# When the output weights' combinations are made in the value stage: units 0 to 3 in place of units 1 to 4

## The chip, the cores and the metric

The kernel runs on one core of one Trainium2 chip. The metric is the device time of one execution in microseconds (us). Engines are named as in the profile: PE (TensorE matmuls), DVE (VectorE), ACT (ScalarE), POOL (GpSimd) and SP (SyncE, which issues most DMAs).

## The reference, cut to what matters

The input is one sequence of 2048 tokens with 1024 features. The output is a gated sum of two blocks of the same input:

```python
g = _sigmoid((x * gate_w).sum(-1, keepdims=True))
a = _A_ref(x, A_wqkv, A_wo)                    # attention: 32 heads of width 32, softmax over 2048 keys
b = _B_ref(x, B_w_q, B_k1, B_k2, B_u, B_v)     # product-key experts, one of 64 for each of 32 heads
return g * a + (1 - g) * b
```

What concerns us here is inside `_A_ref`: the values `v = x @ wqkv[:, 2048:]` (2048x1024 by 1024x1024), and, at the very end, `o @ wo` (2048x1024 by 1024x1024). All matrices are float32.

## The kernel before, in words

**Precision.** Every operand of a large matrix product is split in two parts: ACT copies it to a reduced type (the high part), DVE subtracts that from the original (the low part). That is `split` (line 94; ACT works in line 95, DVE in line 96). A product is then three matmuls for every 128 rows of depth: high by high, high by low, low by high (line 964). So the third matmul of a product is the first that needs the low part of its left operand, and the first one needs its high part.

**Seven products in place of eight.** A block of 256 tokens by 1024 features by 1024 output columns is computed by a Winograd form of Strassen's scheme: both operands are cut into quarters (A11, A12, A21, A22 of the tokens; B11 to B22 of the weights), sums of quarters are made (S1 to S4 of the tokens, T1 to T4 of the weights), and seven products P1 to P7 take the place of eight. Each product is 12 matmuls of 128x128 by 512 columns into one bank of PSUM. DVE then adds the products up to the four quarters C11, C12, C21, C22 of the result.

**Stages.** The kernel first makes queries and keys, then the expert router, then the values (the value stage), then attention over 32 heads (by far the longest part), and finally the output product with `wo`. The output product also uses the scheme with seven products, and so it needs T1 to T4 of `wo`. These do not depend on the data of the other stages. They are made ahead of time during the value stage and are written to DRAM (the tensors `t0h` to `t3l`), from where the last stage reads them back.

**The value stage.** The last 512 tokens are done by plain products before it. The other 1536 are six units of 256 tokens (`values_unit(u)`, line 1144, u = 0 to 5, called from line 1230). The order of the products is P1, P2, P3, P7, P5, P6, P4 in unit 0, and P1, P7, P5, P6, P2, P3, P4 in units 1 to 4. Inside a unit the code is a loop over these seven (k = 0 to 6). All engines work in the order of this code, each on its own list, and an instruction that waits holds up all behind it on its engine. In the loop stand:

- after P1: ACT copies P1 out of PSUM (`c1`, line 1165), and SP issues `load_x_raw(u + 2)`, the 1 MB of tokens of the unit after the next (the *token load*). It goes to one of two buffers, `xw` and a half of the tile `xl`.
- after P6: four sums of products on DVE, then C11 after P2, C12 after P3, C21 after P4 (line 970). Each result goes to DRAM by a DMA that SP issues (`vd`, line 1152).
- the operands of the *next* unit: the high and low parts of A11, the four sums S3, S1, S2, S4 (line 946), and then the splits of S3, S1, S2, A12, S4 and A22, each as soon as the product of this unit that used the same buffer is done. In unit 0 the split of A11 and the sums come at k = 4, the other splits from k = 5 on. In later units they come at k = 0 and from k = 1 on. In the trace the splits that read A11 and A12 write the tile `a`, those of S1 to S4 write `xh`, and that of A22 writes `vo`.
- the *weight work*, which is what the change moves: `load_early(i)` (line 1118) issues four DMAs of 256 KB each on SP (four blocks of `wo`, into the other half of the tile `xl`), `sums_early()` (line 1123) is four sums in place on DVE, and `split_early(i, j)` (line 1130), for j = 0 to 3, is one split each, after which POOL's queue writes both parts to DRAM (`t0h`, `t0l`, `t2h`, `t2l`, `t3h`, `t3l`, `t1h`, `t1l`). There are four rounds, i = 0 to 3. They share one buffer: the load of the next round overwrites what the writes of the last one read. The first sum needs two of the four pieces of a load, the second sum needs the piece that is issued last.

**Banks.** `bank()` (line 110) hands out the eight PSUM banks in turn. A unit takes seven. After each unit up to the fifth one number is left out (line 1241), so that P1 of a unit gets the bank of P1 of the unit before. Between units 1 and 2 there is an exception: `peer_turn` (line 1041) makes four tiles of transposes there, which take four banks more. P1 of unit 2 therefore gets the bank that P2 had in unit 1, and P2's bank becomes free with the sum C11. `peer_turn` also sends four DMAs on SP (`atd<-z`). After their landing, the keys and queries of the first head are loaded by SP (`z<-kdh` and the following ones), and a DVE memset of the same buffer waits for them too (line 1236).

Of the kernel before, what the change touches and what calls it, by code (L numbers as in the profile page):

```python
# [20 lines left out]
HC = KC // 2  # L21
# [10 lines left out]
def gated_mha_peer_kernel(ctx, tc, xT, wqkv, wv, wo, wq, k12, ug, v, out):  # L32
# [42 lines left out]
    def dma(dst, src, queue=nc.sync):  # L75
        a, b = (ap.bitcast(F32) if ap.dtype == F32R else ap for ap in (dst, src))
        return queue.dma_start(a, b)
# [16 lines left out]
    def split(hi, lo, src, on=None):  # L94
        nc.scalar.activation(hi, src, AF.Copy)
        (on or nc.vector).tensor_tensor(out=lo, in0=src, in1=hi.bitcast(F32), op=OP.subtract)
# [872 lines left out]
    def tt(out, a, b, op=OP.add):  # L969
        nc.vector.tensor_tensor(out=out, in0=a, in1=b, op=op)  # L970
# [108 lines left out]
    def load_x_raw(u):  # L1079
        dma(x_raw[u % 2], xT[:, u * W:(u + 1) * W].rearrange("(k p) m -> p k m", p=128))  # L1080
# [37 lines left out]
    def load_early(i):  # L1118
        for j in range(4):
            c0 = (i + j // 2 * HC) * D + j % 2 * 512  # L1120
            dma(early[:, j], wo_rows[:, :, c0:c0 + 512])

    def sums_early():
        b11, b12, b21, b22 = (early[:, j] for j in range(4))
        tt(b11, b12, b11, OP.subtract)
        tt(b12, b22, b12, OP.subtract)
        tt(b22, b22, b11, OP.subtract)
        tt(b21, b21, b22, OP.subtract)

    def split_early(i, j):  # L1130
        hi, lo = work[f"th{j}"].bitcast(F32R), early[:, j].bitcast(F32R)
        split(hi, lo, early[:, j])
        for part, t in enumerate((hi, lo)):

            dma(TD[(0, 2, 3, 1)[j]][part][:, i, :], t, nc.gpsimd)
# [8 lines left out]
    def values_unit(u):  # L1144
        c1, u2, u3, u5 = (work[k] for k in ("c1", "u2", "u3", "u5"))
        last = u == NU - 1
        order = (("P1", "P2", "P3", "P7", "P5", "P6", "P4") if u == 0 else
                 ("P1", "P7", "P5", "P6", "P3", "P2", "P4") if last else
                 ("P1", "P7", "P5", "P6", "P2", "P3", "P4"))
        p, done = {}, set()  # L1150

        def out(j, half, t, queue=nc.sync):
            dma(VD[half][(2 * u + j) * 128:(2 * u + j + 1) * 128, :], t, queue)

        for k, name in enumerate(order):
            if last and name == "P4":

                nonlocal pso
                ps1.close()
                pso = Pool("pso", space=PSUM, side="right")  # L1160
            p[name] = hv.product(name, bank=pv_bank if last and name == "P4" else None)
            if last and name == "P2":
                first_scores()
            if name == "P1":
                nc.scalar.activation(c1, p[name], AF.Copy)
                hv.rows(x_raw[(u + 1) % 2])
                if u + 2 < NU:
                    load_x_raw(u + 2)
            if name == "P6":
                tt(u2, c1, p["P6"])  # L1170
                tt(u3, u2, p["P7"])
                tt(u2, u2, p["P5"])
                tt(u5, u3, p["P5"])
                out(1, 1, u5)
            if "P6" in p:
                if "P2" in p and "C11" not in p:
                    p["C11"] = tt(c1, c1, p["P2"])
                    out(0, 0, c1)
                if "P3" in p and "C12" not in p:
                    p["C12"] = tt(u2, u2, p["P3"])  # L1180
                    out(0, 1, u2)
            if name == "P4":
                tt(u3, u3, p["P4"])

                out(1, 0, u3, nc.gpsimd if last else nc.sync)

            if u + 1 < NU:
                if k == (4 if u == 0 else 0):
                    hv.parts("A11")
                    for s in ("S3", "S1", "S2", "S4"):  # L1190
                        hv.sums(s)
                    done = {"P1"}
                if k >= 5 or u > 0:
                    for q in ("P7", "P5", "P6", "P2", "P3", "P4"):
                        if q in p and q not in done:
                            hv.parts(hv.FACTORS[q][0])
                            done.add(q)
            if 1 <= u <= HC:
                if k == 0:
                    load_early(u - 1)  # L1200
                if k == 3:
                    sums_early()
                for j in {4: (0,), 5: (1,), 6: (2, 3)}.get(k, ()):
                    split_early(u - 1, j)

    P, pools = {}, {}

# [7 lines left out]
    def first_scores():  # L1215

        tp.close()
        pools.update(right=Pool("ppr", side="right"), next=0)
        K, Q = Z
        pt = p_tile(0, 0)  # L1220
        for qc, i in enumerate((5, 6, 0, 1)):
            ps = ps1.tile([128, 512], F32, name=f"bk{i}")
            c = slice(qc * 512, (qc + 1) * 512)
            nc.tensor.matmul(ps, K[:98, :128], Q[:98, c], start=True, stop=True)
            nc.scalar.activation(pt[:, c], ps, AF.Exp, scale=SCALE)
# [4 lines left out]
    for u in range(NU):  # L1230
        values_unit(u)
        if u == 1:
            peer_turn(Ahl)
            for i in range(2):
                Z[i] = zp.tile([128, S], F32R, name=f"z{i}")
            nc.vector.memset(Z[0][96:98, :].bitcast(F32), 1.0)
            load_kq(0, Z)
            load_shift(0, Z)

        if u < 5:  # L1240
            bank_no[0] += 1
# [207 lines left out]
    for h in range(H):  # L1449
        base = h * NT  # L1450
        g, j = divmod(h, 4)
# [319 lines left out]
```

## Time and profile before

| | us |
|---|---|
| median of 3 runs (range) | 1825.43 (1825.37 to 1826.04) |
| the profiled execution, its own time | 1824.19 |
| its span in the trace | 1822.4 |
| value stage, unit 0's first product to unit 5's last scores | 497.48 to 613.94 |
| one unit of seven products | 19.3 |
| PE busy / DVE busy / ACT busy in the span | 1814.7 / 1461.8 / 1312.8 |

The profiled execution's own time is 1.8 us above its span, and 1.2 us below the median of the runs. The timeline rows show, from the left: start, duration, engine, line, operation, the tiles (out<-in), the shape, and how many instructions are merged in the row; a bracket at the end holds idle time before it and what ended that. Consecutive matmuls overlap in such rows, so the time from one start to the next is their rate: 12 matmuls in 2.79 us.

### The profile page before, as it was taken

How to read it: one execution, taken by the hardware profiler on the slowest of the kernel's cores; microseconds unless marked ns; L12 is line 12 of the kernel's file. 1: busy time of each engine (PE TensorE's matmuls, PEld its weight loads, DVE VectorE, ACT ScalarE, POOL GpSimd, SP SyncE). 2: the span in 40 equal slices, each digit the busy share in tenths (PEclk: the TensorE clock that was granted, in tenths of full speed). 3: DMA queues.
4: the chain of work that ended last, by engine and by line, in shares of the span. 5: the costliest groups of instructions: out<-in, count | busy, mean ns of one | idle time of the engine just before them, and what ended most of it. 6: DMA issues, size and time to landing. Idle time of an engine off the chain costs nothing.

```text
span 1822.4 us, 26410 instructions
## 1 busy us (share of the span) xinstructions
PE 1814.7 (100%) x10083; PEld 1099.5 (60%) x10083; DVE 1461.8 (80%) x1258; ACT 1312.8 (72%) x1716; POOL 227.5 (12%) x351
## 2 busy tenths in 40 slices
PE   9999999999999999999999999999999999999999
PEld 6777777788888644444444444444444444447887
DVE  7865876689967888888888888888888888897674
ACT  5544544532333699999999999999999999994221
POOL 1222222244101100000000000000000000000000
PEclk9999999999999999999999999999999999999999
DMA  7888689560267778777788878878787777866641
GB/s 268 277 280 277 215 291 292 191 224 13 81 231 239 232 161 183 157 168 167 166 173 174 181 163 178 171 171 185 165 182 168 163 167 179 185 149 243 252 156 58
DMA packets 117504, 345.23 MB, mean 189 GB/s; under 512 B 16160, under 2 KB 50112, under 8 KB 96448
## 3 DMA queue, kind: packets, MB, share of 16 engines
q1 hardware_dynamic: 87176, 195.37, 36.0%
q0 software_dynamic: 27888, 145.00, 34.4%
q10 hardware_dynamic: 2312, 3.15, 0.5%
q8 instruction: 80, 1.31, 0.3%
q14 instruction: 48, 0.39, 0.1%
HBM read 171.76 MB, written 72.36 MB: 134 GB/s over the span
## 4 chain that ended last, share of the span: by engine, by line
PE 94%; issue 2%; DVE 2%; DMA 1%; ACT 0%; POOL 0%; ACTq 0%; SPq 0%; DVEq 0%; POOLq 0%
PE ring L1318 29%; PE o L1339 26%; PE bk L303 15%; PE pa L964 6%; PE bk L725 5%; PE pa L1521 2%; PE bk L983 2%; PE bk L291 2%; PE bk L964 2%; PE bk L342 2%; PE ring L1352 1%; PE pa L1528 1%; DVE xh L970 1%; DMA t1l<-xl 0%; PE bk L191 0%
## 5 line engine op out<-in xcount | busy, mean ns | idle before, releaser
L1328 ACT ACTIVATE P<-ring 128x1024 f32<-128x1024 f32 (+2 forms) x1031 | 913.0, 984 | 13.3
L1368 DVE TENSOR_TENSOR acc<-acc,P 128x2048 f32<-128x2048 f32 x319 | 731.0, 2292 | 73.3 <-ACT P L1328 48.0
L1339 PE MATMUL o<-P,V 128*32 128x512 f32 x3840 | 464.8, 599 | 0.0
L1318 PE MATMUL ring<-Q,K 98*128 98x512 f32 x1024 | 271.7, 407 | 0.1
L1318 PE MATMUL ring<-z,z 98*128 98x512 f32 x1020 | 270.5, 407 | 0.6 <-ACT accd L1328 0.6
L1318 PEld LDWEIGHTS ring<-Q,K 98*128 98x128 f32 x1024 | 182.2, 188 | 143.6 <-ACT P L1328 73.5
L1318 PEld LDWEIGHTS ring<-z,z 98*128 98x128 f32 x1020 | 181.6, 188 | 142.3 <-ACT P L1328 72.3
L1339 PEld LDWEIGHTS o<-P,V 128*32 128x32 f32 x3840 | 99.0, 109 | 223.3 <-issue 214.4
L1361 POOL DMA_DIRECT2D accd<-P x95 | 81.5, 858 | 928.6 <-PE ring L1318 321.6
L1366 DVE TENSOR_TENSOR acc<-P,P 128x2048 f32<-128x2048 f32 x32 | 73.4, 2293 | 73.8 <-ACT P L1328 73.8
L303 PE MATMUL bk<-xh,A 128*128 128x512 f32 x336 | 82.8, 396 | 0.0
L303 PE MATMUL bk<-xh,S 128*128 128x512 f32 x336 | 81.3, 393 | 0.0
L303 PE MATMUL bk<-xl,S 128*128 128x512 f32 x336 | 80.1, 391 | 0.0
L136 ACT ACTIVATE hi<-u 128x512 fp32r<-128x512 f32 x42 | 26.6, 632 | 70.2 <-issue 39.7
L303 PEld LDWEIGHTS bk<-xh,A 128*128 128x128 f32 x336 | 62.1, 188 | 23.8 <-issue 5.9
L1371 DVE TENSOR_TENSOR acc<-acc,accd 128x2048 f32<-128x2048 f32 x32 | 73.1, 2285 | 0.0
L303 PEld LDWEIGHTS bk<-xl,S 128*128 128x128 f32 x336 | 62.8, 188 | 16.3 <-issue 2.5
L303 PEld LDWEIGHTS bk<-xh,S 128*128 128x128 f32 x336 | 62.4, 188 | 14.5 <-issue 1.7
L1328 ACT ACTIVATE accd<-ring 128x1024 f32<-128x1024 f32 (+2 forms) x64 | 62.3, 1034 | 2.3 <-PE ring L1318 2.2
L964 PE MATMUL pa<-woh,acc 128*128 128x512 f32 x192 | 62.2, 389 | 0.0
L512 DVE TENSOR_TENSOR u<-u,bk 128x512 f32<-128x512 f32 x70 | 46.7, 683 | 10.0 <-DMA wpd<-u 5.6
L729 ACT ACTIVATE xu<-bk 128x64 f32<-128x64 f32 x16 | 3.6, 222 | 61.1 <-PE bk L725 61.1
(301 smaller groups left out, 2209.3 us busy)
## 6 DMA issues: line engine op xcount, KB each, us to landing
accd<-P POOLq DMA_DIRECT2D x95, 1024.0 KB, 7.8
wqt<-in_wq SPq DMA_DIRECT2D x64, 512.0 KB
wraw<-in_wqkv SPq DMA_DIRECT2D x28, 512.0 KB
kdh<-hi POOLq DMA_DIRECT2D x32, 256.0 KB, 5.3
kdl<-lo POOLq DMA_DIRECT2D x32, 256.0 KB, 6.5
qdh<-hi POOLq DMA_DIRECT2D x32, 256.0 KB, 6.0
qdl<-lo POOLq DMA_DIRECT2D x32, 256.0 KB, 5.8
z<-kdh SPq DMA_DIRECT2D x32, 256.0 KB
```

The lines of the kernel that those rows point to most:

```text
L291: nc.tensor.matmul(b0[w, n], AW[PLAIN[w, ki]][a][:, k, :], X[f"B{ki + 1}{n + 1}"][b][:, k, :], start=first, stop=last)
L303: nc.tensor.matmul(ps, a[i][:, k, :], b[j][:, k, :], start=(k == 0 and i == j == 0), stop=(k == HC - 1 and i == 1))
L512: nc.vector.tensor_tensor(out=out, in0=a, in1=b, op=OP.add)
L725: nc.tensor.matmul(ps, x_part(a, t // 4, kc)[:, tok], b, start=first, stop=last)
L964: nc.tensor.matmul(ps, self.a[a][i][:, k, :], self.b[b][j][k], start=(not first and k == 0 and i == j == 0), stop=(k == HC - 1 and i == 1))
L1318: on_ring(nc.tensor.matmul(ring[:, i, :], K[:98, kt * 128:(kt + 1) * 128], Q[:98, qc * 512:(qc + 1) * 512], start=True, stop=True), i)
L1328: on_ring(nc.scalar.activation(P[h, kt][:, q0 * 512:(q0 + m) * 512].rearrange("p (a m) -> p a m", a=m), ring[:, i:i + m, :], AF.Exp, scale ...
L1339: nc.tensor.matmul(O[h][32 * qc:32 * qc + 32, :], Vt[g][:, kt, 32 * j:32 * j + 32], p[:, qc * 512:(qc + 1) * 512], start=(kt == 0), stop=( ...
L1361: nc.gpsimd.dma_start(ACCD[h], P[h, kt], accum_op=OP.add)
L1366: nc.vector.tensor_add(ACC[h], P[h, 0], P[h, kt])
L1368: nc.vector.tensor_add(ACC[h], ACC[h], P[h, kt])
L1371: nc.vector.tensor_add(ACC[h], ACC[h], ACCD[h])
```

## The change

The weight work is done in units 0 to 3 in place of 1 to 4. In the loop of `values_unit`, for unit u, the round is now u, and no longer u - 1:

```diff
-            if 1 <= u <= HC:
+            if u < HC:
                 if k == 0:
-                    load_early(u - 1)
+                    load_early(u)
                 if k == 3:
                     sums_early()
                 for j in {4: (0,), 5: (1,), 6: (2, 3)}.get(k, ()):
-                    split_early(u - 1, j)
+                    split_early(u, j)
```

`HC` is 4. The number of instructions is the same on every engine. Only their order changes, and, for unit 0, their place between the instructions of that unit's own loop order: the four sums come at k = 3, which in unit 0 is after P7 in the code and *ahead* of the split of A11 for unit 1 (k = 4).

The DMA list of SP around unit 0 before the change. `in_xT` are the token loads for units 1, 2 and 3, `vd` the results of unit 0, and the last row is the first load of `wo`:

```order
L77 DMA xl_4614<-in_xT 128x8x256
L77 DMA xw<-in_xT 128x8x256
L77 DMA vd_68<-xh_4594 128x512
L77 DMA vd_67<-xh_4594 128x512
L77 DMA vd_68<-xh_4594 128x512
L77 DMA vd_67<-xh_4594 128x512
L77 DMA xl_4614<-in_xT 128x8x256
L77 DMA xl_4614<-in_wo 128x1x512 x4
```

The same place after the change, up to the second load of `wo`:

```order
L77 DMA xl_4614<-in_xT 128x8x256
L77 DMA xw<-in_xT 128x8x256
L77 DMA xl_4614<-in_wo 128x1x512 x4
L77 DMA vd_68<-xh_4594 128x512
L77 DMA vd_67<-xh_4594 128x512
L77 DMA vd_68<-xh_4594 128x512
L77 DMA vd_67<-xh_4594 128x512
L77 DMA xl_4614<-in_xT 128x8x256
L77 DMA xl_4614<-in_wo 128x1x512 x4
```

A first load of `wo` now stands right behind the token loads for units 1 and 2, ahead of unit 0's results.

DVE's list of unit 0 before, from the low part of A11 for unit 1 (`a_4458`) over the sums S3, S1, S2, S4 (L946) and the sums of products (L970 with a bank `bk`) to the low parts of S3 and S1 (the last row):

```order
L96 TENSOR_TENSOR a_4458<-xl_4614,a_4458 128x512
L946 TENSOR_TENSOR xh_4594<-xl_4614 128x512 x2
L946 TENSOR_TENSOR xl_4614<-xh_4594,xl_4614 128x4x128
L946 TENSOR_TENSOR xl_4614<-xl_4614 128x4x128
L970 TENSOR_TENSOR xh_4594<-xh_4594,bk_4690 128x512
L970 TENSOR_TENSOR xh_4594<-xh_4594,bk_4658 128x512
L970 TENSOR_TENSOR xh_4594<-xh_4594,bk_4671 128x512 x2
L970 TENSOR_TENSOR xh_4594<-xh_4594,bk_4632 128x512
L970 TENSOR_TENSOR xh_4594<-xh_4594,bk_4645 128x512
L96 TENSOR_TENSOR xh_4582<-xh_4594,xh_4582 128x512 x2
```

The same stretch of DVE's list after the change:

```order
L970 TENSOR_TENSOR xl_4614<-xl_4614 128x512 x4
L96 TENSOR_TENSOR a_4458<-xl_4614,a_4458 128x512
L946 TENSOR_TENSOR xh_4594<-xl_4614 128x512 x2
L946 TENSOR_TENSOR xl_4614<-xh_4594,xl_4614 128x4x128
L946 TENSOR_TENSOR xl_4614<-xl_4614 128x4x128
L96 TENSOR_TENSOR xl_4614<-xl_4614,xh_4594 128x512
L970 TENSOR_TENSOR xh_4594<-xh_4594,bk_4702 128x512
L970 TENSOR_TENSOR xh_4594<-xh_4594,bk_4662 128x512
L970 TENSOR_TENSOR xh_4594<-xh_4594,bk_4679 128x512 x2
L970 TENSOR_TENSOR xh_4594<-xh_4594,bk_4636 128x512
L970 TENSOR_TENSOR xh_4594<-xh_4594,bk_4649 128x512
L96 TENSOR_TENSOR xh_4582<-xh_4594,xh_4582 128x512 x2
```

Two pieces of weight work stand in it now: the four sums of `wo` at its head (the first row), and the low part of the first split ahead of the sums of products (the sixth row).

## The prediction

> **What bounds the kernel now.** I read the head of the page first, then the chain that ended last, then PE's waits in the value stage, and only then the engines' lists there.
>
> ```profile
> span 1822.4 us, 26410 instructions
> PE 1814.7 (100%) x10083; PEld 1099.5 (60%) x10083; DVE 1461.8 (80%) x1258; ACT 1312.8 (72%) x1716; POOL 227.5 (12%) x351
> PE 94%; issue 2%; DVE 2%; DMA 1%; ACT 0%; POOL 0%; ACTq 0%; SPq 0%; DVEq 0%; POOLq 0%
> ```
>
> PE is busy for 1814.7 of 1822.4 us, and the chain is 94% PE. The change takes no matmul away. So it can win only what PE waits now, and lose whatever new waits it makes for PE. PE's waits between 470 and 640 us, which hold the value stage and the start of attention (waited for; us in total, times, longest):
>
> ```profile
> PE ring L1318 <- ACT accd L1328: 0.6, 1, 0.6
> PE bk L1224 <- DVE xh L970: 0.5, 1, 0.5
> ```
>
> Both lie behind unit 5. Units 0 to 5 themselves run without a wait, so moving the weight work earlier has at most 1.1 us to win, and only if both vanish. What it can lose is the question. The PE rows to which everything is compared are P1 and P7 (with P5) of unit 1, P1 of unit 2, and P2 of unit 4:
>
> ```profile
> 516.76 2.96 PE L964 MATMUL bk<-xh,a 128*128 128x512 f32 x12
> 519.56 5.61 PE L964 MATMUL bk<-vt,xh 128*128 128x512 f32 x24
> 537.75 3.03 PE L964 MATMUL bk<-xh,a 128*128 128x512 f32 x12
> 587.42 2.96 PE L964 MATMUL bk<-xl,a 128*128 128x512 f32 x12
> ```
>
> **Step 1: when the first load of `wo` lands.** SP's rows in unit 0 (token loads for units 1 and 2), in unit 1 (token load, then today's first load of `wo`) and in unit 3 (the same pair), and the DMA engines in four stretches (the last two numbers of a row are their busy share and GB/s):
>
> ```profile
> 501.95 0.39 SPq L77 DMA_DIRECT2D xl<-in_xT  x1
> 504.36 0.37 SPq L77 DMA_DIRECT2D xw<-in_xT  x1
> 522.33 0.38 SPq L77 DMA_DIRECT2D xl<-in_xT  x1
> 522.77 2.70 SPq L77 DMA_DIRECT2D xl<-in_wo  x4
> 569.33 0.38 SPq L77 DMA_DIRECT2D xl<-in_xT  x1
> 569.80 11.07 SPq L77 DMA_DIRECT2D xl<-in_wo  x4
> ...
> 504.50:512.25 7.75, 7.75 (x36) 6.43 (x35) 2.45 (x4) 2.92 (x5) 0.00 (x0) 1.00 1.06 382
> 512.50:514.00 1.50, 1.50 (x9) 1.22 (x8) 0.62 (x1) 0.06 (x1) 0.00 (x0) 1.00 0.00 1
> 522.50:529.75 7.25, 7.25 (x33) 5.97 (x32) 5.94 (x10) 1.90 (x3) 0.00 (x0) 1.00 0.94 325
> ```
>
> After the change the load is issued behind the token load of 504.36, so in a stretch where the DMA engines are full (382 GB/s) until about 512.3. It moves 4 x 128 x 512 x 4 bytes = 1.05 MB, at 382 GB/s 2.7 us more: its traffic ends at 515.0. In unit 1 today the traffic of such a pair ends at 529.75 and the sums start at 531.19 without a wait, so landing is told at most 1.4 us after the traffic. I take 0.6, so the second sum, which needs the last piece, starts at **515.6**; bounds 515.0 (no lag) and 516.4 (the whole 1.4).
>
> **Step 2: what DVE then makes late.** DVE's rows for unit 0 (the low part of A11 for unit 1, the four sums S, the six sums of products, the low parts of S3 and S1), then today's first sums of `wo`, and the sum C11 of unit 1:
>
> ```profile
> 509.77 0.69 DVE L96 TENSOR_TENSOR a<-xl,a 128x512 fp32r<-128x512 f32 x1 [5.43 <-ACT a L95]
> 510.38 1.29 DVE L946 TENSOR_TENSOR xh<-xl 128x512 f32<-128x512 f32 x2
> 512.42 0.69 DVE L946 TENSOR_TENSOR xl<-xl 128x512 f32<-128x512 f32 x1
> 514.17 3.92 DVE L970 TENSOR_TENSOR xh<-xh,bk 128x512 f32<-128x512 f32 x6 [1.05 <-PE bk L964]
> 518.01 1.29 DVE L96 TENSOR_TENSOR xh<-xh,xh 128x512 fp32r<-128x512 f32 x2
> ...
> 531.19 2.87 DVE L970 TENSOR_TENSOR xl<-xl 128x512 f32<-128x512 f32 x4
> 533.97 0.68 DVE L970 TENSOR_TENSOR xh<-xh,bk 128x512 f32<-128x512 f32 x1
> ```
>
> Today A11's low part starts at 509.77. Afterwards it stands behind the four sums of `wo`, which wait for the load. The rows of unit 2's round, quoted below, give 2.06 us from the second sum to the next instruction (562.35 to 564.41), so A11's low part starts at 517.7. From there: A11 and the four sums S, 509.77 to 513.1, are 3.3; the low part of the first split of `wo`, new here, 0.6; the six sums of products, 514.17 to 518.01, 3.84; the low part of S3 0.69. It is done at 517.7 + 3.3 + 0.6 + 3.84 + 0.69 = 526.1. P7 of unit 1 needs it in its third matmul, 24 matmuls taking 5.45 us, so at 519.56 + 0.46 = 520.0. **PE is 6.1 us late** (bounds 5.5 and 6.9 by step 1). Of these, 1.2 are lost already at P1, since A11 is done at 518.4 and due at 517.2. The cover that hides this work today is that DVE reaches A11 7 us before PE; the four sums' wait eats all of it. S1, S2, A12, S4 follow S3 every 0.6 us and PE needs them every 2.8 us or less often: no more there.
>
> **Step 3: the second round and the bank.** P1 of unit 2 gets the bank that C11 of unit 1 frees. Today that is at 534.6 and P1 starts at 537.75: cover 3.1 us. Afterwards unit 1 has the round i = 1, whose load must wait until the writes of round 0 have read the buffer. No row shows this round in unit 1, but unit 3 today has the same company: a token load, then a load of `wo` behind the last round's writes, so that SP needs 11.07 us for its four issues. The waits of SP between 490 and 640 us, the landing times of the last write, and DVE's rows in units 2 and 3 (second to fourth sum, C11 and the low part of A12, then first sum, second to fourth sum and A12):
>
> ```profile
> SPq L77 <- DMA t3l<-xl: 7.1, 2, 6.1
> DMA to landing us min/median/max: 3.2/5.0/9.0
> 562.35 2.14 DVE L970 TENSOR_TENSOR xl<-xl 128x512 f32<-128x512 f32 x3 [1.86 <-DMA xl<-in_wo]
> 564.41 0.68 DVE L970 TENSOR_TENSOR xh<-xh,bk 128x512 f32<-128x512 f32 x1
> 565.01 0.68 DVE L96 TENSOR_TENSOR a<-xl,a 128x512 fp32r<-128x512 f32 x1
> 580.62 0.69 DVE L970 TENSOR_TENSOR xl<-xl 128x512 f32<-128x512 f32 x1 [2.41 <-DMA xl<-in_wo]
> 583.82 2.15 DVE L970 TENSOR_TENSOR xl<-xl 128x512 f32<-128x512 f32 x3 [2.51 <-DMA xl<-in_wo]
> 586.48 0.69 DVE L96 TENSOR_TENSOR a<-xw,a 128x512 fp32r<-128x512 f32 x1
> ```
>
> There the second sum starts 583.82 - 569.33 = 14.5 us after the token load. Afterwards S3's low part starts at 525.4; seven instructions later, 0.6 us each, comes A22's, done at 530.3, and the token load for unit 3 is issued at 530.4. That would give 544.9. As unit 0's other results have left by then, I take 544.0. The lower bound has the last write land in the median 5.0 and not in 9.0 us: 540.9. C11 follows 2.06 later and takes 0.69: 546.8. P1 of unit 2 is due at 537.75 + 6.1 = 543.9. **Another 2.9 us** (0 to 3.8).
>
> **Step 4: rounds 2 and 3.** The result C21 of unit 1 leaves six DVE slots after C11's start, at 550.4. `atd` stands behind it on SP, and behind `atd` the loads of keys and queries:
>
> ```profile
> 538.69 3.49 SPq L77 DMA_DIRECT2D atd<-z  x4
> 546.49 0.80 SPq L77 DMA_DIRECT2D z<-kdh  x2
> 546.98 1.76 DVE L1236 MEMSET z<- 2x2048 f32 x1 [6.92 <-DMA atd<-z]
> ```
>
> C21's own issue takes 0.4 us, from the first `atd` to those loads are 7.8 today, and from them to the second sum 15.9 (to 562.35): 550.4 + 24.1 = 574.5. The next round's comes 21.5 later (562.35 to 583.82), at 596.0, and A12 is done 3.35 after that, at 599.3. P2 of unit 4 needs it at 587.42 + 0.46 today, with 0.7 us to spare, and at 597.0 with steps 2 and 3. **Another 2.3 us** (0 to 3.3). Unit 4 has no weight work any more, so DVE catches up, and the wait of 0.5 us behind unit 5 goes: **-0.5** (0 to -1.1). What else moves costs nothing: ACT's splits of `wo` stand beside DVE's and ACT is 28% idle; POOL's writes have POOL to themselves; `wo`'s T1 to T4 are read only by the last stage.
>
> **The sum.** 6.1 + 2.9 + 2.3 - 0.5 = 10.8 us on the profiled execution's 1824.2, so 1835.0; the median of the runs lies 1.2 above that execution, and I forecast **1836.2**. The bounds are 5.5 - 1.1 = +4.4 (1829.8) and 6.9 + 3.8 + 3.3 = +14.0 (1839.4).
>
> **The rivals.** *Only the first wait counts*: landings are quick, DVE has caught up by unit 2, and the sum is 6.1 - 0.5: 1831. For it speaks that DVE idles for 6.9 us in unit 2 today; against it, that this idling is itself a wait for DMA. *Covered*: pieces of the load of `wo` overtake the token load, the second sum starts by 511, A11's low part by 513.1, and S3's is done by 521.5; the writes of each round land in 5 us or less, so that steps 3 and 4 stay within their cover. Then 1.5 us remain, less up to 1.1 at the end: 1826, not slower. It decides if the load lands before 511; the traffic that is full until 512.25 speaks against it. *PE's clock falls in the new pauses*: in step 2 PE stands idle from 520.9, P1's end, to the sum C11 of unit 0 at 524.9, 4.0 us. The end of the kernel and its start show what such a pause does (the seventh column of the second row is the granted clock):
>
> ```profile
> 1818.02 0.39 PE L964 MATMUL pa<-woh,acc 128*128 128x512 f32 x1
> 1821.00:1822.40 1.40, 0.00 (x0) 0.00 (x0) 0.00 (x0) 0.00 (x0) 0.00 (x0) 0.52 0.00 0
> 1.40 4.50 PE L409 MATMUL bk<-ident 128*128 128x128 f32 x22 [1.40 <-DVE ident L91]
> 536.08 1.91 PE L1045 MATMUL bk<-ident,z 128*128 128x128 f32 x16
> ```
>
> 2.6 us after the last matmul the clock is at half. At the start 22 small matmuls take 0.20 us each and in the stage 0.12, so after a pause up to 4.5 us of work go at about half speed and lose some 2 us. After the first pause step 3's wait hides that, as C11 of unit 1 is held by DMA and not by PE. After the second pause (2.9 us) it would show: 1838, and with the upper bounds 1841. [...]
>
> **How the numbers follow.** My forecast with all of its waits (1832 to 1839.5) 0.64; first wait alone (1829.8 to 1832) 0.14; clock or longer landings on top (to 1842) 0.11; covered 0.11, of which all but 0.02 lie within 0.2% (3.7 us), which is about what a measurement of this kernel can tell from no change. Slower by more: 0.64 + 0.14 + 0.11 = 0.89, less 0.01 for the first case's edge. The range for 8 in 10 is 1829.5 to 1840.5, which takes in the bounds and half of the last case.
>
> **What would show it.** DVE in unit 0 idle until about 515 for `xl<-in_wo`; PE rows that wait for DVE `xh` and `a` in unit 1, P1 of unit 2 at about 547 after a wait for DVE L970, P2 of unit 4 waiting for A12; the span of units 0 to 5 longer by 10 us and everything behind it equal. A first sum of `wo` before 511, or P7 of unit 1 starting within 1 us of 519.6, would prove step 1 or 2 wrong.

## The result, and the profile after

The kernel after takes **1836.96 us** (median of 6 runs, 1835.83 to 1838.09) against 1825.74 us (6 runs, 1825.23 to 1827.08) of the kernel before on the same chip: a ratio of 1.0061, 95% interval 1.0051 to 1.0072. That is 11.2 us more. The forecast was 10.8 more. The profiled execution, at 1838.09 us, is the slowest of the six.

The span is 1836.3 us, and no instruction is added. PE's waits between 470 and 640 us (waited for; us in total, times, longest):

```profile
PE bk L964 <- DVE xh L970: 4.0, 1, 4.0
PE bk L964 <- ACT xu L95: 3.1, 2, 2.6
PE bk L964 <- DVE a L96: 1.0, 1, 1.0
```

Where there was one wait of 0.5 us, there are now four with 8.1 us together, all inside the value stage, and the wait behind unit 5 (L1224) is gone. PE's timeline shows them in their places: P2 of unit 0; P1 of unit 1 (in two pieces); P7 with P5, and P6, of unit 1; P1 and P7 with P5 of unit 2; P2 of unit 4; the first product behind the scores of unit 5.

```profile
502.28 2.96 PE L964 MATMUL bk<-xl,a 128*128 128x512 f32 x12
...
518.76 0.62 PE L964 MATMUL bk<-xh,a 128*128 128x512 f32 x2
520.41 2.58 PE L964 MATMUL bk<-xh,a 128*128 128x512 f32 x10 [1.03 <-DVE a L96]
526.99 7.50 PE L964 MATMUL bk<-vt,xh 128*128 128x512 f32 x24 [4.00 <-DVE xh L970]
534.33 2.89 PE L964 MATMUL bk<-xh,xh 128*128 128x512 f32 x12
...
549.87 4.51 PE L964 MATMUL bk<-xh,a 128*128 128x512 f32 x12 [2.55 <-ACT xu L95]
554.18 5.74 PE L964 MATMUL bk<-vt,xh 128*128 128x512 f32 x24
...
601.86 3.10 PE L964 MATMUL bk<-xl,a 128*128 128x512 f32 x12 [0.58 <-ACT xu L95]
...
627.81 2.96 PE L964 MATMUL o<-xl,vo 128*128 128x512 f32 x12
```

The same places in the kernel before that stand in no row above are P2 of unit 0, P6 of unit 1 and P7 with P5 of unit 2:

```profile
500.27 2.96 PE L964 MATMUL bk<-xl,a 128*128 128x512 f32 x12
...
525.01 2.89 PE L964 MATMUL bk<-xh,xh 128*128 128x512 f32 x12
...
540.61 5.61 PE L964 MATMUL bk<-vt,xh 128*128 128x512 f32 x24
```

In this execution the value stage begins 2.01 us later than in the profiled execution of before (P2 of unit 0 at 502.28 against 500.27 there), by something ahead of it that the change does not touch. The rows stay as the profile has them, but where times of two kernels are compared they are put on **before's clock**, by subtracting the difference at P2 of unit 0 (2.01 here). So P7 of unit 1 is 526.99 - 2.01 - 519.56 = 5.4 late, P6 7.3 (before had it at 525.01), P1 of unit 2 10.1, its P7 11.6 (540.61), P2 of unit 4 12.4, and the first product behind the scores 11.9 (613.94). Nothing is added behind that.

DVE shows what PE waited for: the four sums of round 0, the low part of A11, the sums of products and S3; then the second sums of round 1 with C11 of unit 1, and the same of unit 3:

```profile
516.35 0.69 DVE L970 TENSOR_TENSOR xl<-xl 128x512 f32<-128x512 f32 x1 [10.02 <-DMA xl<-in_wo]
517.60 2.15 DVE L970 TENSOR_TENSOR xl<-xl 128x512 f32<-128x512 f32 x3 [0.56 <-DMA xl<-in_wo]
519.67 0.68 DVE L96 TENSOR_TENSOR a<-xl,a 128x512 fp32r<-128x512 f32 x1
523.53 3.91 DVE L970 TENSOR_TENSOR xh<-xh,bk 128x512 f32<-128x512 f32 x6
527.36 1.29 DVE L96 TENSOR_TENSOR xh<-xh,xh 128x512 fp32r<-128x512 f32 x2
...
546.98 2.14 DVE L970 TENSOR_TENSOR xl<-xl 128x512 f32<-128x512 f32 x3 [3.17 <-DMA xl<-in_wo]
549.04 0.68 DVE L970 TENSOR_TENSOR xh<-xh,bk 128x512 f32<-128x512 f32 x1
...
598.98 2.14 DVE L970 TENSOR_TENSOR xl<-xl 128x512 f32<-128x512 f32 x3 [2.34 <-DMA xl<-in_wo]
601.04 0.68 DVE L970 TENSOR_TENSOR xh<-xh,bk 128x512 f32<-128x512 f32 x1
```

DVE stands 10 us before the first sum, with the split of A11 and all of unit 0's sums behind it. Further down, C11 (549.04) ends at 549.72, and P1 of unit 2 starts 0.15 later. The waits list names "ACT xu" there, but that is only the last of several semaphores by the profile: in the five experiments below in which P1 of unit 2 waits, its start is also 0.14 to 0.15 us behind the end of C11, whatever ACT does. The same holds at P2 of unit 4 (601.72 and 601.86). It is the bank that PE waits for.

SP's timeline has the token load that is issued in unit 1 and the four issues of round 1's load behind it:

```profile
532.28 0.39 SPq L77 DMA_DIRECT2D xl<-in_xT  x1
532.77 11.30 SPq L77 DMA_DIRECT2D xl<-in_wo  x4
```

The list of DMA issues between 525 and 548 us has the writes of round 0, with the median time to landing as the last number. Here is the last of them, first in this kernel and then in the kernel before, where no token load stands beside it:

```profile
t1l<-xl POOLq DMA_DIRECT2D x1, 256.0 KB, 9.3
...
t1l<-xl POOLq DMA_DIRECT2D x1, 256.0 KB, 5.2
```

The second sums were late because the four issues take 11.3 us: SP waits until the writes have read the buffer. The last write of 256 KB is issued 1.9 us behind the token load of 532.28 and needs 9.3 us, where it needed 5.2 in the kernel before.

One more thing shows in the rows of PE: 24 matmuls of P7 take 7.50 us in place of 5.61, and 12 of P1 4.51 in place of 3.03. The granted clock (the third number from the right) around the two:

```profile
527.00:528.00 1.00, 1.00 (x2) 0.36 (x2) 1.00 (x3) 0.00 (x0) 0.00 (x0) 0.55 0.90 348
530.00:531.00 1.00, 1.00 (x5) 0.82 (x4) 1.00 (x3) 0.14 (x1) 0.00 (x0) 0.74 0.00 0
...
550.00:551.00 1.00, 1.00 (x5) 0.82 (x6) 1.00 (x3) 1.00 (x3) 0.00 (x0) 1.00 0.43 170
551.00:552.00 1.00, 1.00 (x4) 0.75 (x3) 1.00 (x2) 1.00 (x3) 0.78 (x2) 0.50 0.25 92
...
554.00:555.00 1.00, 1.00 (x5) 0.78 (x5) 1.00 (x2) 0.58 (x2) 0.27 (x2) 0.79 0.93 361
```

It is at half from about 527.1 to 530.5, and from 551.0 to about 554.4, although PE has been at work again since 549.87.

### The profile page after: what moved, and what is told of

It reads as the page before. It is cut to its first block, busy times and chain, and to the rows that moved or that the text cites. A ratio compares the mean times of both kernels' runs of the same rounds, so it can differ in the third digit from the quotient of the medians.

```text
span 1836.3 us, 26410 instructions
## 1 busy us (share of the span) xinstructions
PE 1820.0 (99%) x10083; PEld 1100.3 (60%) x10083; DVE 1461.9 (80%) x1258; ACT 1312.3 (71%) x1716; POOL 227.6 (12%) x351
## 3 DMA queue, kind: packets, MB, share of 16 engines
q10 hardware_dynamic: 2312, 3.15, 0.5%
## 4 chain that ended last, share of the span: by engine, by line
PE 93%; issue 3%; DMA 2%; DVE 1%; POOL 1%; ACT 1%; SPq 0%; DVEq 0%; POOLq 0%; ACTq 0%
PE ring L1318 28%; PE o L1339 26%; PE bk L303 15%; PE pa L964 6%; PE bk L725 5%; PE pa L1521 2%; PE bk L983 2%; PE bk L291 2%; PE bk L342 2%; PE ring L1352 1%; PE bk L964 1%; PE pa L1528 1%; DMA xl<-in_wo 0%; DMA t1l<-xl 0%; PE bk L191 0%
## 5 line engine op out<-in xcount | busy, mean ns | idle before, releaser
L512 DVE TENSOR_TENSOR u<-u,bk 128x512 f32<-128x512 f32 x70 | 46.6, 682 | 11.2 <-DMA wpd<-u 7.1
```

Source lines behind the costliest of these rows:

```text
L512: nc.vector.tensor_tensor(out=out, in0=a, in1=b, op=OP.add)
```

## The experiments

The theory after the result: two chains set the time. In unit 0, DVE's list holds A11, the sums of products and S3 behind the first load of `wo`. In unit 1, the bank for P1 of unit 2 stands behind C11, that behind round 1's second sums, those behind the load, and the load behind the token load and the writes of round 0. Rivals: the new traffic in unit 0 as such; the clock; DVE simply having too much work in units 0 to 3. Every kernel was compared with runs of the kernel before on the same chip, which took 1825.42 us (25 runs) beside the first four kernels below, 1825.46 (13) beside *sums behind A11 alone* and the last one, and 1825.48 (22) beside the others. The diffs are against the kernel after.

### The load alone

```diff
-            if u < HC:
-                if k == 0:
-                    load_early(u)
-                if k == 3:
+            if u <= HC:
+                if k == 0 and u != 1:
+                    load_early(max(u - 1, 0))
+                if k == 3 and u > 0:
                     sums_early()
-                for j in {...}.get(k, ()):
-                    split_early(u, j)
+                for j in {...}.get(k, ()) if u > 0 else ():
+                    split_early(u - 1, j)
```

> Only the DMAs of the first load of wo are moved to unit 0; all sums, splits and writes stay in units 1 to 4 as before. My theory says that the place of the load costs nothing and DVE's order does: the time of the kernel before within 0.5 us, A11's split in unit 0 at the same place, no new wait on PE. Rival (traffic: 1 MB more behind the token loads of unit 0 makes A11 or the results late): 2 to 5 us slower with PE waits in unit 1.

It took 1825.15 us (1823.96 to 1825.69), ratio 0.9999 (0.999 to 1.0009). PE's only wait up to the scores:

```profile
PE bk L1224 <- DVE xh L970: 1.4, 1, 1.4
```

1 MB more in the busiest stretch of unit 0 costs nothing. The rival of the new traffic in unit 0 falls. What costs is the instructions that stand behind the load.

### Round 0 alone, with and without work in the pause

The first kernel does round 0 in unit 0 and rounds 1 to 3 in units 2 to 4. The second adds 16 matmuls ahead of P7 of unit 1 whose results nothing reads.

```diff
-            if u < HC:
+            if u <= HC and u != 1:
+                i = max(u - 1, 0)
                 if k == 0:
-                    load_early(u)
+                    load_early(i)
...
-                    split_early(u, j)
+                    split_early(i, j)
...
+            if u == 1 and name == "P7":
+                fill(16, bank_no[0] - 2)
```

> Round 0 of the weight work in unit 0 as in the changed kernel, rounds 1 to 3 in units 2 to 4 as in the kernel before; unit 1 has none. My theory (the four sums stand ahead of A11's split on DVE and wait for their load): P7 of unit 1 starts 5.4 us late as in the changed kernel, the clock halves in that pause and P6 of unit 1 is 7.3 us late; C11 of unit 1 is not behind any sums of wo, so nothing is added at P1 of unit 2; unit 4 keeps its work and the 0.5 us behind unit 5 stay. Sum: 7.3 us over the kernel before, about 1833. Rival (the moved traffic makes the loads late everywhere): the delay grows on in units 1 to 4, 9 us or more. Rival (the clock costs nothing of its own): 5.4 us, 1831.

> The same as e1_round0_alone, and 16 matmuls (128x128 by 512, 3.7 us) more on PE between P1 and P7 of unit 1, into the bank that is idle there; nothing reads their result. They lie in PE's pause of 4.0 us. If the pause halves the clock and the lost 1.9 us stand in the time: 1.9 us faster than e1_round0_alone, granted clock 1.00 through units 1 and 2, P6 of unit 1 5.4 us late. If the 7.3 us of e1 are waiting alone: no faster than e1, or slower by the matmuls that do not fit.

They took 1832.26 us (1831.7 to 1832.91; ratio 1.0036, 1.0022 to 1.0050) and 1830.41 us (1829.71 to 1831.76; 1.0025, 1.0015 to 1.0036): 6.8 and 5.0 above before, both near what was expected (7.3 above, and 1.9 less with the matmuls). P7 of unit 1 and P1 of unit 2 with the first kernel, and with the second the added matmuls, P7 in two pieces, and P6:

```profile
526.44 8.14 PE L964 MATMUL bk<-vt,xh 128*128 128x512 f32 x24 [3.99 <-DVE xh L970]
...
547.15 3.03 PE L964 MATMUL bk<-xh,a 128*128 128x512 f32 x12
```

```profile
522.46 3.82 PE L1147 MATMUL bk<-xh 128*128 128x512 f32 x16
526.62 0.70 PE L964 MATMUL bk<-vt,xh 128*128 128x512 f32 x2 [0.34 <-DVE xh L970]
527.72 5.28 PE L964 MATMUL bk<-vt,xh 128*128 128x512 f32 x22 [0.40 <-DVE xh L96]
532.84 2.89 PE L964 MATMUL bk<-xh,xh 128*128 128x512 f32 x12
```

Without a round in unit 1, P1 of unit 2 waits for nothing: step 3 belongs to the second round. With PE busy in the pause, P7's 24 matmuls go at full speed, and P6 stands at 532.84 - 1.67 (P2 of unit 0 at 501.94) = 531.17, which is 6.16 late: step 2 without the clock, forecast as 6.1. The 1.85 us between the two kernels are the clock: its mean in the profiled executions is 0.998 and 1.0.

### The sums and splits of round 0 at the end of unit 0

```diff
-                if k == 3:
+                if k == (6 if u == 0 else 3):
...
-                for j in {4: (0,), 5: (1,), 6: (2, 3)}.get(k, ()):
+                for j in ({6: (0, 1, 2, 3)} if u == 0 else {...}).get(k, ()):
```

> The changed kernel with the sums and the four splits of round 0 at the end of unit 0's list (k = 6, behind all splits for unit 1); rounds 1 to 3 as in the changed kernel. My theory: DVE does not wait in unit 0, P7 of unit 1 starts on time, and only the second part is left: round 1's load waits for round 0's writes, so that C11 of unit 1 comes at about 538.6 (on the clock of the profile of before) and P1 of unit 2 is 1 us late, P2 of unit 4 about 1 us more, less 0.7 at the end: 1 to 2 us over the kernel before, 1827. Rival (DVE simply has too much to do in units 0 and 1, wherever it stands): still 5 us or more over it.

It took 1829.74 us (1828.6 to 1831.38; ratio 1.0026, 1.0016 to 1.0035), 4.3 above before, so the size was missed. P7 of unit 1 and P1 of unit 2:

```profile
520.62 5.61 PE L964 MATMUL bk<-vt,xh 128*128 128x512 f32 x24
...
542.21 4.58 PE L964 MATMUL bk<-xh,a 128*128 128x512 f32 x12 [3.15 <-ACT xu L95]
```

The wait at P7 is gone, as the theory says, and the one at P1 of unit 2 has grown to 3.15 us with a fall of the clock behind it. All eight writes of round 0 now stand at the end of unit 0's work, issued one behind another from 524.93 to 530.26; the next load, issued from 530.63 on, stands behind them until 536.5 (5.83 us for its four issues). So C11 of unit 1 starts at 541.38 and ends at 542.06, 541.0 on before's clock (1.07 subtracted), and not near 538.6.

### The next load let go

```diff
-            dma(TD[(0, 2, 3, 1)[j]][part][:, i, :], t, nc.gpsimd)
+            dma(TD[(0, 2, 3, 1)[j]][part][:, i, :], hi if i == 0 else t, nc.gpsimd)
```

> The kernel after, except that the writes of the low part of round 0's four pieces read the tile of the high part, so that nothing but the splits themselves reads the buffer into which the next token load goes; the number and size of the transfers stay. The low parts written for round 0 are those of the high part, so the output is not the reference's. My theory (the next load stands behind the writes that still read the buffer, the three sums behind the load, the add of unit 1 behind the sums): round 1's load starts some 3 us earlier, round 1's second sums no longer wait 3.17 us, P1 of unit 2 waits for nothing of it; whole time some 3.4 us below the kernel after: 1833.5 us, 1832 to 1834.5. Rival (traffic, or VectorE's own work, holds the chain, not the write before the load): as after, 1837 us, within 0.7.

It took 1832.17 us (1831.23 to 1832.69; ratio 1.0037, 1.0024 to 1.0051), 4.8 below the kernel after. Round 1's sums on DVE with C11, and P1 of unit 2 on PE:

```profile
539.11 2.86 DVE L970 TENSOR_TENSOR xl<-xl 128x512 f32<-128x512 f32 x4
541.89 0.68 DVE L970 TENSOR_TENSOR xh<-xh,bk 128x512 f32<-128x512 f32 x1
```

```profile
545.26 3.03 PE L964 MATMUL bk<-xh,a 128*128 128x512 f32 x12
```

The sums wait for nothing and C11 ends 2.7 us before PE wants the bank. More than the expected 3.4 us went, since the second fall of the clock (1.45) goes with the pause of 2.55 that caused it. But the kernel changes two things: as the writes of the low parts no longer wait for DVE's splits, the last one is issued 6.6 us earlier and needs 5.0 us, not 9.3. Whether the hold or the collision with the token load weighs more is not told apart by it. The order of the loads, below, leaves the hold and takes the collision away, though it also brings the first load in earlier.

### Both pauses filled

```diff
+            if u == 1 and name == "P7":
+                fill(16, bank_no[0] - 2)
...
             peer_turn(Ahl)
+            fill(16, bank_no[0])
```

> The kernel after with two sets of 16 matmuls whose results nothing reads, one in TensorE's wait ahead of P7 of unit 1, one in its wait ahead of P1 of unit 2. Both theories: granted clock 1.00 in all of the value stage. My theory (the two clock losses of 1.9 and 1.45 us lie inside waits that VectorE's and the loads' chain sets): P1 of unit 2 starts as late as in the kernel after, the wait at P2 of unit 4 grows from 0.6 to about 2 us, the whole time is that of the kernel after within 0.5 us, 1836.5 to 1837.5. Rival (the losses of the clock add to the sum): 3.3 us less, 1833.7.

It took 1836.4 us (1836.07 to 1836.98; ratio 1.0061, 1.0046 to 1.0077), within 0.6 of the kernel after. P7, P1 of unit 2 and its P7, and P2 of unit 4:

```profile
526.04 5.28 PE L964 MATMUL bk<-vt,xh 128*128 128x512 f32 x22 [0.40 <-DVE xh L96]
...
548.61 3.04 PE L964 MATMUL bk<-xh,a 128*128 128x512 f32 x12 [0.83 <-ACT xu L95]
551.48 5.61 PE L964 MATMUL bk<-vt,xh 128*128 128x512 f32 x24
...
599.20 3.10 PE L964 MATMUL bk<-xl,a 128*128 128x512 f32 x12 [0.75 <-ACT xu L95]
```

All matmuls go at full speed (granted clock 1.00 from 516 to 532 and from 544 to 556 us), and yet the end stays: the clock's losses lie inside waits that the chain of loads and sums sets. The wait at P2 of unit 4 grew less than expected (0.58 to 0.75, not 2), because in this execution round 1's second sum came 0.9 us later on before's clock (545.84 against 544.97), so that at P7 of unit 2 PE had kept only 0.6 us of the gain: SP's four issues of round 1's load, which wait for round 0's writes, took 12.11 us here, not 11.30.

### The weights' load ahead of the token load, and the sums behind A11: all four cases

The first edit issues the load of `wo` ahead of the token load in each unit. The second, in unit 0, puts the three sums behind the split of A11 and the sums S1 to S4, and the splits of the parts one step later.

```diff
+                if u < HC:
+                    load_early(u)
                 if u + 2 < NU:
                     load_x_raw(u + 2)
...
-                if k == 0:
-                    load_early(u)
```

```diff
-                if k == 3:
+                if k == (4 if u == 0 else 3):
...
-                for j in {4: (0,), 5: (1,), 6: (2, 3)}.get(k, ()):
+                for j in ({5: (0, 1), 6: (2, 3)} if u == 0 else {...}).get(k, ()):
```

> The kernel after, but SP issues the output weights' token load and its loads ahead of the next raw load of tokens in each unit, not behind it. My theory (the pause is set by when round 0's load lands and by the load after it, not by the amount of work in units 0 to 3): round 0's load lands 2.6 to 3 us earlier, P7 of unit 1 is some 2.4 us late in place of 5.4 without loss of clock, no wait for it at P1 of unit 2 nor at P2 of unit 4, and 0.7 us is gained at the end: 1827.2 us, 1826 to 1829. Rival (VectorE has too much to do in those units, whatever the order of the loads): 1835 us or more.

> The kernel after, with the loads where they are there, and in unit 0 only the sums behind the split of A11 and the sums S, and the splits of the parts one step later. Together with the kernels that have one or both of the two cures it gives all four cases. My theory (each cure takes one wait away: the place of the sums the wait at P7 of unit 1, the order of the loads the one at P1 of unit 2): P7 of unit 1 some 2 us late, as the sums end at 517.7 on the clock of the trace of before and the six sums of products stand behind them; then round 1's token load still stands ahead of its weights' load, the second sum comes near 542, and P1 of unit 2 waits 3 to 5 us with a loss of clock behind it; 0.7 us gained at the end: 1832.5 us, 1830.5 to 1834.5. Rival (once nothing that TensorE needs stands behind the first load, the order of the loads no longer matters): 2 us late at P7 and no more, 1827 us.

> As the kernel with the weights' load first, and in unit 0 the three sums stand behind the sums S and the splits of A11, with the splits of the parts one step later, so that nothing that TensorE waits for in unit 1 stands behind the load. My theory: P7 of unit 1 is at most 0.5 us late, no other wait is added, 0.7 us is gained at the end: 1825.5 us, 1825 to 1827, not to be told from the kernel before. Rival (the later splits bring the wait back at P1 of unit 2, as where the sums stood in the late place of unit 0): 1829 us or more.

| | median (range), us | ratio to before | P7 of unit 1 late | C11 of unit 1 starts |
|---|---|---|---|---|
| before | 1825.48 (1824.05 to 1826.93) | 1 | 0 | 534.0 |
| after | 1836.96 (1835.83 to 1838.09) | 1.0061 (1.0051 to 1.0072) | 5.4 | 547.0 |
| sums behind A11 alone | 1835.08 (1835.02 to 1835.27) | 1.0056 (1.0039 to 1.0073) | 2.3 | 545.5 |
| load first alone | 1829.45 (1827.91 to 1831.38) | 1.0021 (1.0012 to 1.003) | 3.4 | 541.4 |
| both | 1825.34 (1824.23 to 1826.69) | 1.0 (0.9991 to 1.0009) | 0 | 538.1 |

The last two columns are on before's clock; subtracted are 2.01, 0.23, 0.73 and -0.36 us from *after* to *both*. The times and ratio of *after* are those of the result above. The rows of the case with the sums behind A11 alone (P7 of unit 1, and P1 of unit 2), of the load first alone (P7 of unit 1, P1 of unit 2), and of both (the same):

```profile
522.10 0.70 PE L964 MATMUL bk<-vt,xh 128*128 128x512 f32 x2 [2.15 <-DVE xh L970]
...
546.57 5.42 PE L964 MATMUL bk<-xh,a 128*128 128x512 f32 x12 [5.25 <-ACT xu L95]
```

```profile
523.72 0.70 PE L964 MATMUL bk<-vt,xh 128*128 128x512 f32 x2 [3.27 <-DVE xh L970]
524.82 6.87 PE L964 MATMUL bk<-vt,xh 128*128 128x512 f32 x22 [0.41 <-DVE xh L96]
...
544.27 3.03 PE L964 MATMUL bk<-xh,a 128*128 128x512 f32 x12
```

```profile
520.15 5.28 PE L964 MATMUL bk<-vt,xh 128*128 128x512 f32 x22 [0.33 <-DVE xh L96]
...
538.51 3.03 PE L964 MATMUL bk<-xh,a 128*128 128x512 f32 x12 [0.27 <-ACT xu L95]
```

*Both* came out as expected, and so the rival that DVE has too much work in units 0 to 3 falls: the same work in the same units costs nothing if PE does not come to need what stands behind a load before the load has landed (C11 of unit 1 still stands behind one, and ends just in time). *Sums behind A11 alone* missed upward (1832.5 expected, at most 1834.5): it halves the wait at P7, but P1 of unit 2 then waits 5.25 us in place of 2.55, since C11 hardly moved (545.5 against 547.0), and the longer pause costs 2.4 us of clock (5.42 against 3.03 for P1). What PE gains ahead of a milestone (a time that another chain sets) is lost at the milestone. *Load first alone* took 4.0 above before, where 1.7 was expected: the second sum came at 513.6 on before's clock, 2.0 us earlier than in the kernel after and not 2.6 to 3, and behind the pause the clock was at half (0.61 on the mean from 524 to 528 us). The last run asked whether that clock accounts for the miss.

### Load first, with work in the pause

The edit is that of the load first together with the 16 unread matmuls ahead of P7 of unit 1.

> The kernel with the weights' load first, and 16 matmuls whose results nothing reads in TensorE's wait ahead of P7 of unit 1. It asks what the 2.3 us are by which that kernel came out longer than I had expected. My theory (1.7 us of them are the clock, which its pause of 3.3 us halved): granted clock 1.00 in all of the value stage, P6 of unit 1 some 1.7 us earlier, and nothing behind it that takes the gain back, so 1.7 us less than that kernel: 1827.8 us, 1827 to 1828.6. Rival (the pause itself is longer because the load lands later, and the clock's loss is hidden by a later wait): no change, 1829.5 us.

It took 1829.76 us (1828.14 to 1831.55; ratio 1.0024, 1.0014 to 1.0034): no change, and my expectation was wrong. The rival's time came out, though not for both of its reasons: the load landed no later (second sum at 513.0 on before's clock, against 513.6), but a later wait took the gain. P7 of unit 1 and P1 of unit 2:

```profile
523.66 5.62 PE L964 MATMUL bk<-vt,xh 128*128 128x512 f32 x24
...
543.66 3.03 PE L964 MATMUL bk<-xh,a 128*128 128x512 f32 x12 [1.56 <-ACT xu L95]
```

P7 runs at full speed, and P1 of unit 2 then waits 1.56 us for C11. So here the bank is the milestone, 5.4 us late (543.66 - 0.47 - 537.75). Without the matmuls it was not: there C11 ended at 542.84, and P1 of unit 2 started 1.4 us later, at 544.27 (5.8 late), because PE itself was late by its pause and the clock. That the two kernels take the same time rests on C11, which with the matmuls started at 542.4 on before's clock, 0.9 us later than the 541.4 without them. It came later behind slower writes: SP's four issues of round 1's load, which wait for them, took 10.22 us, against 8.03. Each profile shows one execution, and these two kernels spread over 3.4 and 3.5 us between runs (all others over 0.3 to 2.9), so why the writes were slower is open.

## Why the prediction was right, step by step

- **Step 1** held: the second sum at 517.60 - 2.01 = 515.59, forecast 515.6.
- **Step 2** held: S3's low part is done at 527.36 + 0.69 - 2.01 = 526.04, forecast 526.1, and P6 without the clock is 6.16 late, forecast 6.1. P1's share was 1.03 (1.2).
- **Step 3** had the right mechanism, and a choice in it was wrong. The token load went out at 530.27 (530.4), and 14.7 us later came the second sum, at 544.97. The working had given 544.9; I took 544.0, "as unit 0's other results have left by then". The rows do not bear that out: the last write needed 9.3 us. So P1 of unit 2 was 10.1 late, not 9.0.
- **The clock** was a rival with 0.11. Its 2 us were taken from the start of the kernel, which does not show a half clock (1.00 from 0 to 8 us in the kernel before); the end does (0.52 from 1821.0 to 1822.4). It did fall behind both pauses (to 0.50, for 3.41 us each), but the time of that rival, 1838 as an addition to the sum, did not come. After the first pause it cost P6 some 1.2 us in the profile (7.3 against 6.1), which step 3 hid, as the text said; after the second 1.45, which it priced on top. That second loss was no addition to the whole, since step 4's wait shrank by it. The working had 2.9 us for the second pause; it was 2.55.
- **Step 4** was mis-sized: 2.3 forecast (2.4 by its own terms, since 587.42 + 0.46 + 9.0 is 596.9 and not 597.0), 0.9 measured (12.4 - 11.6). The chain itself was forecast within 1.4 us: the second sum of round 2 at 575.85 (574.5), that of round 3 at 596.97 (596.0). But PE was already 11.6 late by the clock and step 3, so less was left to wait. And it waited for C11's bank; A12's low part (601.63 + 0.68) just came in time for the third matmul.
- **The end**: the wait of 0.5 us is gone, and 12.43 - 11.86 = 0.6 came back (0.5).

So 6.1 + 2.9 + 2.3 - 0.5 = 10.8 stood against 7.3 + 2.8 + 1.45 + 0.9 - 0.6 = 11.9 in the profile and 11.2 between the medians. The sum came near because a milestone that DMA and DVE set does not care how PE spends the time ahead of it: what the clock took after the second pause is what step 4's wait lacked. P2 of unit 4, forecast 11.3 late, was 12.4 late in the profile: the 1.1 between them are about what the choice of 544.0 in step 3 left out (0.97). That 10.8 lies within 0.4 of the medians' difference is in part luck, since the profiled execution, in which the steps are read, gives 11.9.

No version beat both kernels. PE's waits in before leave 1.1 us to win, 0.06%, less than such a comparison can show. The one with both edits gains the wait at the end and gives it back in waits of 0.33 and 0.27 in its profile.

## What to carry to other kernels

When work with a load at its head is moved earlier, look at what stands behind it on the in-order engine: the load alone cost nothing, its first consumer ahead of A11 cost 5 to 7 us, and at the end of unit 0's list it cost P7 nothing, but 4.3 us in all by the bank behind it. With the sums behind A11 and the load first, the same move cost nothing (1825.34 against 1825.48). A chain through DMA, a sum and a bank is a milestone whose time PE does not set; gains and losses ahead of it do not add up, so work out its time and compare, and do not sum waits. And the order of two loads on one queue counts where the writes that hold the second one back compete with the first (9.3 us to the last one's landing, and 5.3 with the load first): 7.5 us here, in which the first load's landing 2.0 us earlier is contained.

## What the runs showed of the hardware

- **Pauses of 2.55, 3.15, 3.27, 3.99, 4.00 and 5.25 us went with a half clock or with slow matmuls; those of 2.15 and 1.56 did not.** In the kernel after, the granted clock was 0.50 for 3.41 us twice, behind the pause of 4.00 us (527.1 to 530.5; PE back at 526.99) and behind that of 2.55 us (551.0 to 554.4; PE back at 549.87). With the load first alone it was at half from about 524.8 to 528.3, behind the pause of 3.27 us (PE back at 523.72). With the sums behind A11 alone it was at half from about 545.0 to 551.8, from within the pause of 5.25 us on (PE back at 546.57). In two kernels the matmuls show it: behind the pause of 3.15 us 12 of them took 4.58 us in place of 3.03, and with round 0 alone, behind the one of 3.99 us, 24 took 8.14 us in place of 5.61. With the sums behind A11 alone the clock was 1.00 from 520 to 528 us, behind the pause of 2.15 us (PE back at 522.10), and with the load first and work in the pause 12 matmuls took 3.03 us behind the one of 1.56 us.
- **The half clock did not begin or end with the pause.** It began 0.1 and 1.1 us after PE was back at work in the kernel after and 1.1 us after with the load first alone, and 1.6 us before PE was back with the sums behind A11 alone. It lasted 3.4 us in the first three cases and 6.8 us in the last. What sets its beginning and its length is not shown.
- **The time of a write to landing** differed with what was issued beside it. The last of round 0's eight writes of 256 KB took 9.3 us in the kernel after, where it was issued 1.9 us behind a token load of 1 MB. It took 5.2 us in the kernel before and 5.0 with the next load let go, where none was issued just ahead of it. In the kernel with the load of `wo` first:

```profile
t1l<-xl POOLq DMA_DIRECT2D x1, 256.0 KB, 5.3
```
